# A weight transfer changes queue: the lower half of w_in's second piece goes to ScalarE's queue, and the gate weights go to GpSimd's

## The chip, the cores and the metric

The kernel runs on one core of a Trainium2 chip. A core has a matrix engine (TensorE, PE in the profile), a vector engine (VectorE, DVE), a scalar engine (ScalarE, ACT), a general engine (GpSimd, POOL) and an engine that only issues transfers and waits (SyncE, SP). Each has its own instruction stream, taken in order; they meet at semaphores. Transfers between the device memory and the on-chip memory are issued by instructions in the streams of SP, ACT or POOL, and are carried out by the core's 16 DMA engines.

The metric is the device time of one execution in microseconds (us).

## The reference: what is computed

Two branches read the same x (2048 tokens by 512 features, bf16), and a gate mixes them token by token:

```
g = sigmoid((x * gate_w).sum(-1))
a = linear attention of x: q, k, v = x @ wqkv; per head softmax features of q and k,
    kv = phi_k^T v, o = (phi_q kv) / (phi_q z), a = o @ wo
b = z = gelu(x @ w_in)  (2048 x 1376), split in z1 and z2; z2 is layer-normed,
    multiplied by the 2048 x 2048 matrix w_sp, plus b_sp; b = (z1 * that) @ w_out
out = g * a + (1 - g) * b
```

The change touches only how two inputs are brought in: `w_in` (512 x 1376) and `gate_w` (512 values).

## The kernel before, in words

The order of all work is written out by hand; the framework adds the semaphores. Tokens are worked in 16 tiles of 128. First comes z = x @ w_in for all tiles, with gelu on ScalarE and the statistics of the layer norm on VectorE; then the attention features and the large product with w_sp; then the outputs. The change and everything that the prediction speaks of lie in the first 20 us, in the z stage.

**What a z tile needs.** The contraction over 512 features is cut in four slices of 128 (`dt` 0 to 3). The 1376 columns of w_in are cut in three pieces: columns 0 to 511, 512 to 1023, and 1024 to 1375 with one further column F that holds the gate weights, so that the same matmuls also give x . gate_w. `z_piece` (L177, matmul at L180) does one piece of one tile. Tiles 0 and 1 are taken side by side and start early: their x comes by a plain load (L108, L109), is transposed on TensorE (`x_transpose`, L195) and copied out by VectorE for tile 0 (L204) and by ScalarE for tile 1 (L206). The other x tiles come by transposing transfers (L123, L129).

**The order on TensorE at the start** is: 24 matmuls on constants (`spin`, L189), the two x transposes, four more on constants, then for tiles 0 and 1 in turn, slice by slice: columns 0 to 255, columns 256 to 511, the gate column's small matmul (`gate_column`, L209), columns 512 to 1023. After that comes the third piece of tile 0, that of tile 1, and tiles 2 to 15. VectorE copies the four gate values of each row into column F of w_in (L212). This copy writes into the same tile as the third piece's load and is ordered behind it; the third piece's matmuls read column F and so wait for the copy.

**The transfers of w_in.** For short they have names here. Each is one call of `load_w_in` (L111), save d:

| name | what | KB | queue before |
|---|---|---|---|
| a, a' | columns 0-255, slices 0-1 and slices 2-3 | 128 each | SP, ScalarE |
| b, b' | columns 256-511, slices 0-1 and slices 2-3 | 128 each | SP, ScalarE |
| c, c' | columns 512-1023, slices 0-1 and slices 2-3 | 256 each | SP, SP (L119) |
| d | columns 1024-1375, all slices (L122) | 352 | SP |

SP's queue holds, in this order: x tile 0, a, b, c, c', d, the transposing load of x tiles 2 and 3 (L123), wv (L124), more x (L129), and so on. ScalarE's queue holds x tile 1, a', b', the gate weights gw (L120, 1 KB), and much later the outputs. After its transfers ScalarE runs a small gelu that loads its tables (L121). GpSimd's queue holds no transfer at all; GpSimd builds the identity (L101, L102), clears a part of w_out (L153), builds masks (L162 to L167) and clears paddings (L173, L174). VectorE's first instruction (L175) adds two halves of a mask and waits for L167.

**Completion counters.** The framework gives the transfers of the SP and ScalarE queues eight completion semaphores in turn. A ninth transfer takes the first one's, and its issue waits until that first one has landed. Before the change the eight are x tile 1, x tile 0, a', a, b', b, gw and c; so c' is the ninth and waits for x tile 1, and d the tenth, which waits for x tile 0.

Of the kernel before, what the change touches and what calls it, by code (L numbers as in the profile page):

```python
# [14 lines left out]
P = 128  # L15
# [9 lines left out]
CH = 512  # L25
# [14 lines left out]
def kernel(  # L40
# [14 lines left out]
    nc = tc.nc  # L55
# [11 lines left out]
    def zbank(t):  # L67
# [32 lines left out]
    gw = pers.tile([NDT, P], BF16, name="gw")  # L100
    nc.gpsimd.memset(ident[:], 1.0)  # L101
    nc.gpsimd.affine_select(  # L102
        out=ident[:], in_=ident[:], pattern=[[-1, P]],
# [7 lines left out]
    def load_w_in(eng, d0, d1, n0, n1):  # L111
        eng.dma_start(out=w_in[:, d0:d1, n0:n1], in_=w_in_v[:, d0:d1, n0:n1])  # L112

    HC = CH // 2
    for n0 in (0, HC):
        load_w_in(nc.sync, 0, 2, n0, n0 + HC)
        load_w_in(nc.scalar, 2, 4, n0, n0 + HC)
    for d0 in (0, 2):
        load_w_in(nc.sync, d0, d0 + 2, CH, 2 * CH)  # L119
    nc.scalar.dma_start(out=gw[:], in_=gate_w.rearrange("(dt p) -> dt p", p=P))  # L120
    nc.scalar.activation(out=st[:, 9, 0:1], in_=ones[:, 0:1], func=AF.Gelu_apprx_tanh)  # L121
    nc.sync.dma_start(out=w_in[:, :, 2 * CH:F], in_=w_in_v[:, :, 2 * CH:F])  # L122
    nc.sync.dma_start_transpose(out=xT[:, :, 2 * P:CH], in_=x2[2 * P:CH, :])  # L123
# [1 line left out]
        out=wv[:, :, :],  # L125
        in_=A_wqkv[:, 2 * D:3 * D].rearrange("(dt p) n -> p dt n", p=P),
    )
    for q in range(1, NCH):
        nc.sync.dma_start_transpose(  # L129
            out=xT[:, :, q * CH:(q + 1) * CH], in_=x2[q * CH:(q + 1) * CH, :]  # L130
        )
        if q == 1:
            nc.sync.dma_start(
                out=wphiW[:, :, :],
                in_=A_w_phi.rearrange("(g h) e f -> (h e) g f", g=NDT),
# [3 lines left out]
        out=bcolb[:, :, :], in_=B_b_sp.rearrange("(t p) -> t p", p=P)  # L139
# [7 lines left out]
    for t in range(WSLOTS):  # L147
        load_wsp(t)
    nc.sync.dma_start(
        out=w_out[:, 0:NFT - 1, :],  # L150
        in_=B_w_out[0:(NFT - 1) * P, :].rearrange("(ft p) n -> p ft n", p=P),
# [4 lines left out]
        out=w_out[0:last_m, NFT - 1, :], in_=B_w_out[(NFT - 1) * P:FH, :]  # L156
    )
    nc.sync.dma_start(
        out=wo[:, :, :], in_=A_wo.rearrange("(g p) n -> p g n", p=P)
# [4 lines left out]
        out=mask16[:], in_=mask16[:], pattern=[[-16, 8]],  # L164
# [3 lines left out]
        out=mask16[:], in_=mask16[:], pattern=[[16, 8]],  # L168
# [420 lines left out]
```

## Time and profile before

| | us |
|---|---|
| median of 3 runs | 208.01 (208.0 to 208.05) |
| the profiled execution | 208.12 |
| its span (first to last instruction) | 206.4 |
| TensorE busy in the span | 202.3 (98%) |
| VectorE busy | 148.5 (72%) |
| ScalarE busy | 82.1 (40%) |
| GpSimd busy | 49.5 (24%) |

The profile shows one execution. "Busy" is the sum of an engine's instructions; a group's line gives the code line, the engine, the operation, its tiles and its count. The chain is followed back from the last instruction, at each step to what released it. The timeline gives start, duration, engine and line; "SPq" and "ACTq" are transfer issues on the SP and ScalarE queues, and the time to landing in the list of transfers runs from the start of the issue until all of the data is there.

### The profile page before, as it was taken

To read this page: it belongs to the slowest core of one execution; us is meant where nothing else is said; L and a number is where in the kernel's file an instruction comes from. 1 tells how busy PE (TensorE), PEld (TensorE's weight loads), DVE (VectorE), ACT (ScalarE), POOL (GpSimd) and SP (SyncE) were. 2 spreads that over 40 slices of the span, in tenths; PEclk is the share of its full clock that TensorE was granted. 3 is DMA by queue.
4 is the path that set the end of the run, shared out by engine and by line. 5 is a ranking of instruction groups with operands and counts; after the bars stand their busy time and mean duration, and the time that the engine had idled before them with its cause. 6 is when DMAs were issued, how large, how long until landed. Compare 5 with 4: busy or idle time off the path is not lost.

```text
span 206.4 us, 3685 instructions
## 1 busy us (share of the span) xinstructions
PE 202.3 (98%) x1399; PEld 117.8 (57%) x1399; DVE 148.5 (72%) x304; ACT 82.1 (40%) x145; POOL 49.5 (24%) x46
## 2 busy tenths in 40 slices
PE   8999999999999999999999999999999999999994
PEld 8545555554455666666666667666455555555542
DVE  1049858385887888879898996798989788796500
ACT  4266767675684324250505102222524243341122
POOL 4000000000002353525352543032532252322000
PEclk9999999999999999999999999999999999999999
DMA  5999899997000638463757781145756974566451
GB/s 160 289 178 247 189 170 226 168 192 231 0 3 0 140 65 117 102 112 85 153 126 109 139 174 41 38 91 84 161 131 122 127 176 98 129 141 153 110 110 51
DMA packets 90378, 26.50 MB, mean 128 GB/s; under 512 B 84296, under 2 KB 90360, under 8 KB 90360
## 3 DMA queue, kind: packets, MB, share of 16 engines
q1 hardware_dynamic: 87360, 23.87, 60.2%
q10 hardware_dynamic: 3000, 2.39, 3.8%
q8 instruction: 11, 0.18, 0.4%
q14 instruction: 7, 0.06, 0.1%
HBM read 3.44 MB, written 2.10 MB: 27 GB/s over the span
## 4 chain that ended last, share of the span: by engine, by line
PE 96%; DMA 2%; SPq 0%; ACT 0%; issue 0%
PE ps L405 36%; PE ps L180 18%; PE ps L326 13%; PE ps L448 10%; PE ps L453 7%; PE ps L282 7%; DMA w_in<-in_B_w_in_dram 2%; PE ps L427 2%; PE ps L377 2%; PE ps L305 1%; SPq L112 0%; SPq L108 0%; ACT ob L457 0%; PE ps L209 0%
## 5 line engine op out<-in xcount | busy, mean ns | idle before, releaser
L405 PE MATMUL ps<-zz,wsp 128*128 128x344 bf16 x512 | 84.1, 309 | 0.0
L343 POOL TENSOR_TENSOR w_in<-w_in,rs 128x512 bf16<-128x512 bf16 x28 | 41.3, 1475 | 124.7 <-DVE rs L341 112.4
L405 PEld LDWEIGHTS <-wsp 128*128 128x128 bf16 x512 | 49.9, 98 | 28.1
L334 ACT ACTIVATE w_in<-ps 128x512 bf16<-128x512 f32 x56 | 30.1, 596 | 63.3 <-issue 21.4
L180 PE MATMUL ps<-w_in,xT 128*128 128x512 bf16 (+2 forms) x200 | 39.7, 350 | 0.4 <-DMA w_in<-in_B_w_in_dram 0.4
L339 DVE TENSOR_REDUCE zs<-w_in 128x64 f32<-128x1024 bf16 x28 | 33.8, 1209 | 0.0
L413 DVE SCALAR_TENSOR_TENSOR u<-ps,bcol,zz 128x344 bf16<-128x344 f32 x32 | 18.4, 574 | 18.6 <-PE ps L427 8.3
L180 PEld LDWEIGHTS <-xT 128*128 128x128 bf16 x200 | 19.1, 98 | 18.0 <-issue 0.8
L215 ACT ACTIVATE zz<-ps 128x1376 bf16<-128x1376 f32 (+2 forms) x18 | 21.4, 1190 | 18.6 <-PE ps L180 18.6
L448 PE MATMUL ps<-w_out,uT 128*128 128x512 bf16 (+2 forms) x102 | 23.5, 366 | 0.0
L224 DVE BATCH_NORM_STATS2 stats<-zz 128x6 f32<-128x344 bf16 x32 | 14.8, 505 | 11.1 <-ACT zz L215 11.1
L377 PE MATMUL ps<-vv,w_in 128*128 128x65 bf16 x128 | 21.7, 193 | 0.0
L343 DVE TENSOR_TENSOR w_in<-w_in,rs 128x512 bf16<-128x512 bf16 x28 | 19.4, 693 | 1.0
L341 DVE RECIPROCAL rs<-zs 128x64 f32<-128x64 f32 x32 | 17.7, 553 | 3.2
L457 ACT ACTIVATE ob<-ps 128x512 bf16<-128x512 f32 (+2 forms) x17 | 9.7, 572 | 25.1 <-PE ps L453 19.9
L453 PE MATMUL ps<-wo,oT 128*128 128x512 bf16 (+2 forms) x68 | 16.6, 366 | 0.0
L326 PEld LDWEIGHTS <-xT 128*128 128x128 bf16 x128 | 10.8, 98 | 9.9
L326 PE MATMUL ps<-wq,xT 128*128 128x512 bf16 x64 | 16.4, 379 | 0.0
L326 PE MATMUL ps<-wk,xT 128*128 128x512 bf16 x64 | 16.3, 379 | 0.0
L427 PE MATMUL ps<-kvx,wqkT 128*128 128x68 bf16 x128 | 15.8, 194 | 0.0
L282 PE MATMUL ps<-wv,xT 128*128 128x512 bf16 x64 | 15.6, 379 | 0.0
L448 PEld LDWEIGHTS <-uT 128*128 128x128 bf16 x102 | 9.5, 98 | 10.4
(56 smaller groups left out, 134.3 us busy)
## 6 DMA issues: line engine op xcount, KB each, us to landing
out_dram<-ob ACTq DMA_DIRECT2D x15, 128.0 KB, 2.1
w_out<-in_B_w_out_dram SPq DMA_DIRECT2D x1, 640.0 KB, 4.9
w_in<-in_B_w_in_dram SPq DMA_DIRECT2D x2, 256.0 KB, 4.5
wv<-in_A_wqkv_dram SPq DMA_DIRECT2D x1, 512.0 KB, 5.0
wo<-in_A_wo_dram SPq DMA_DIRECT2D x1, 512.0 KB, 5.3
w_in<-in_B_w_in_dram SPq DMA_DIRECT2D x1, 352.0 KB, 4.9
w_in<-in_B_w_in_dram ACTq DMA_DIRECT2D x2, 128.0 KB, 4.0
w_in<-in_B_w_in_dram SPq DMA_DIRECT2D x2, 128.0 KB, 3.6
```

Of the source, the lines that this page charges most:

```text
L180: nc.tensor.matmul(zb[:, n0:n1], lhsT=xT[:, dt, t * P:(t + 1) * P], rhs=w_in[:, dt, n0:n1], start=(dt == 0), stop=(dt == NDT - 1),)
L215: nc.scalar.activation(out=zz[:, t, n0:n1], in_=zbank(t)[:, n0:n1], func=AF.Gelu_apprx_tanh)
L282: nc.tensor.matmul(ps[:, b, :], lhsT=xT[:, dt, t * P:(t + 1) * P], rhs=wv[:, dt, :], start=(dt == 0), stop=(dt == NDT - 1),)
L326: nc.tensor.matmul(ps[:, b, :], lhsT=xT[:, dt, t * P:(t + 1) * P], rhs=w[:, dt, :], start=(dt == 0), stop=(dt == NDT - 1),)
L334: nc.scalar.activation(out=e[:, :, a, :], in_=src, func=AF.Exp, scale=sc)
L339: nc.vector.tensor_reduce(out=zs[:], in_=ev, axis=AX.X, op=ALU.add)
L343: eng.tensor_tensor(out=ev[:, sl, :], in0=ev[:, sl, :], in1=rs[:, sl, None].to_broadcast([P, H, DH]), op=ALU.mult,)
L377: nc.tensor.matmul(slots[:, g, 0:HW + 1], lhsT=ek_t[t][:, g, :, :].rearrange("p a n -> p (a n)"), rhs=vv[:, t, g, 0:HW + 1], start=(t == 0 ...
L405: nc.tensor.matmul(ps[:, b, 0:HF], lhsT=wsp[:, tt % WSLOTS, s, :], rhs=zz[:, s, FH + h * HF:FH + (h + 1) * HF], start=(s == 0), stop=(s == ...
L427: nc.tensor.matmul(slots[:, g, 0:QW], lhsT=eT_t[t][:, g, :], rhs=kvx[:, g, :], start=True, stop=True)
L448: nc.tensor.matmul(ps[:, b, n0:n1], lhsT=uT[:, ft, :], rhs=w_out[:, ft, n0:n1], start=(ft == 0), stop=False,)
L453: nc.tensor.matmul(ps[:, b, n0:n1], lhsT=oT[:, g, :], rhs=wo[:, g, n0:n1], start=False, stop=(g == NDT - 1),)
```

## The change

The second piece of w_in was loaded by two transfers on SP's queue. Now its upper half c stays there, and its lower half c' becomes the fourth transfer on ScalarE's queue, where gw stood. The gate weights are issued on GpSimd's queue, whose first transfer they are; in GpSimd's stream the issue stands behind the identity and ahead of L153.

```diff
     for n0 in (0, HC):
         load_w_in(nc.sync, 0, 2, n0, n0 + HC)
         load_w_in(nc.scalar, 2, 4, n0, n0 + HC)
-    for d0 in (0, 2):
-        load_w_in(nc.sync, d0, d0 + 2, CH, 2 * CH)
-    nc.scalar.dma_start(out=gw[:], in_=gate_w.rearrange("(dt p) -> dt p", p=P))
+    load_w_in(nc.sync, 0, 2, CH, 2 * CH)
+    load_w_in(nc.scalar, 2, 4, CH, 2 * CH)
+    nc.gpsimd.dma_start(out=gw[:], in_=gate_w.rearrange("(dt p) -> dt p", p=P))
     nc.scalar.activation(out=st[:, 9, 0:1], in_=ones[:, 0:1], func=AF.Gelu_apprx_tanh)
     nc.sync.dma_start(out=w_in[:, :, 2 * CH:F], in_=w_in_v[:, :, 2 * CH:F])
```

No arithmetic changes, and no transfer changes its size.

## The prediction

> **What bounds the kernel now.** The page's chain of what ended last comes first: 96% of the span is TensorE, 2% transfers, all of it w_in. So only what lets TensorE start or continue earlier can pay, and only in the stretch where it waits for w_in. The same chain in order of time, for the first 30 us, shows that stretch:
>
> ```profile
> 1.72 4.46 DMA w_in<-in_B_w_in_dram
> 6.18 0.04 issue
> 6.22 1.05 PE ps L180 x8
> 7.28 0.10 PE ps L209
> 7.38 12.50 PE ps L180 x64
> ```
>
> TensorE waits until 6.18 for one transfer issued at 1.72 (b), and from 6.22 on the chain stays on TensorE. The waits of the same window say how much idle time that is, and where else w_in is waited for:
>
> ```profile
> DVE w_in L212 <- DMA w_in<-in_B_w_in_dram: 4.1, 1, 4.1
> PE ps L180 <- DMA w_in<-in_B_w_in_dram: 0.4, 1, 0.4
> PEld L180 <- DMA w_in<-in_B_w_in_dram: 0.2, 1, 0.2
> SPq L112 <- DMA xn<-in_A_x_dram: 0.8, 1, 0.8
> ```
>
> TensorE is idle 0.43 us ahead of b. The gate column's copy on VectorE waits for d. SP's issue of c' waits 0.8 us for an x tile (the ninth transfer's counter). The timeline of the issues, and the transfers with their time to landing:
>
> ```profile
> 1.73 0.51 ACTq L112 DMA_DIRECT2D w_in<-in_B_w_in_dram  x1
> 2.27 0.62 ACTq L120 DMA_DIRECT2D gw<-in_gate_w_dram  x1
> ...
> 2.22 0.47 SPq L112 DMA_DIRECT2D w_in<-in_B_w_in_dram  x1
> ...
> 3.54 0.37 SPq L112 DMA_DIRECT2D w_in<-in_B_w_in_dram  x1
> ...
> 3.96 0.47 SPq L122 DMA_DIRECT2D w_in<-in_B_w_in_dram  x1
> 4.47 1.95 SPq L123 DMA_TRANSPOSE xT<-in_A_x_dram  x1
> ```
>
> ```profile
> w_in<-in_B_w_in_dram SPq DMA_DIRECT2D x1, 256.0 KB, 4.8
> w_in<-in_B_w_in_dram SPq DMA_DIRECT2D x1, 128.0 KB, 4.5
> w_in<-in_B_w_in_dram ACTq DMA_DIRECT2D x1, 128.0 KB, 4.9
> ...
> w_in<-in_B_w_in_dram SPq DMA_DIRECT2D x1, 352.0 KB, 4.9
> w_in<-in_B_w_in_dram SPq DMA_DIRECT2D x1, 256.0 KB, 4.3
> ```
>
> Issue plus time to landing: b 6.18, b' 1.73 + 4.9 = 6.63, c 2.22 + 4.8 = 7.02, c' 3.54 + 4.3 = 7.84, d 3.96 + 4.9 = 8.86. Against this the needs on TensorE. The second piece's matmuls start at 7.31 and then every 0.216 us (8 of them, two a slice): c is needed at 7.31, c' (slices 2 and 3) at 7.31 + 4 x 0.216 = 8.17. The third piece could start at 7.31 + 8 x 0.216 = 9.04; it starts at 9.19, because VectorE's copy, released by d, runs from 8.96 to 9.14. So there are 0.29 us of slack on c, 0.33 on c', and 0.15 us of waiting behind d. The last line to read is the rate of the 16 DMA engines, by stretches:
>
> ```profile
> 3.50:5.50 2.00, 2.00 (x20) 1.82 (x19) 0.82 (x3) 1.63 (x5) 0.00 (x0) 1.00 0.93 244
> 5.50:6.60 1.10, 0.67 (x7) 0.45 (x6) 0.00 (x0) 0.00 (x0) 0.00 (x0) 1.00 1.00 314
> 6.60:7.00 0.40, 0.40 (x5) 0.33 (x4) 0.00 (x0) 0.00 (x0) 0.00 (x0) 1.00 1.06 358
> ```
>
> The third number from the right is the granted clock, the next the busy share of the DMA engines, the last GB/s: they are full (0.93 to 1.06) when c, c' and d move. The wait is for bytes, not for an issue.
>
> **The change, part by part.**
>
> SP's queue loses c' (0.37 us of issue). Without gw on the ScalarE queue, the first eight counters are x tile 1, x tile 0, a', a, b', b, c' and c: none of these waits, and d is now the ninth, released by x tile 1's landing. So d is issued at 3.54 instead of 3.96 and all that SP issues behind it (x tiles 2 and 3, wv, the later x, w_phi, wqk) up to 0.42 us earlier. With the DMA engines full until d has landed, an earlier issue brings no earlier byte: 0. The x tiles 2 and 3 land at 4.47 + 5.4 = 9.87, ahead of their first use at 9.19 + 8 x 0.15 = 10.39; those 0.52 us cover them, and without them a later landing would count in full. wv is first read at 19.72.
>
> ScalarE's queue loses gw (0.62 us of issue) and gains c' (0.46 to 0.51, the rows of its own w_in issues): its table load starts about 0.13 us earlier, at 2.79 for 2.92. Its next work, tile 1's copy at 4.45, waits for the transposes on TensorE, which end at 4.41: 0. SP had four transfers out (x, a, b, c) before any had landed, so a fourth on ScalarE's queue need not block its stream.
>
> c' enters its queue at 2.27 instead of 3.54, behind b' and no longer behind c. This is the edit that counts. From 6.63, when b' is down, c needed 0.39 us more, then c' 0.82 (256 KB, 320 GB/s), then d 1.02. Now c and c' run together. If the engines alternate between the two queues, c takes 2 x 0.39 and lands at 7.41, 0.39 later; c' has 0.43 us of work left, shares with d, and lands at 7.41 + 0.86 = 8.27, 0.43 later; d, whose engines have moved the same bytes in all, lands at 8.86 as before. On TensorE: c at 7.41 moves the second piece's start from 7.31 to 7.45 (0.04 from landing to start, as at b), 0.14 late; c' is then needed at 8.31 and there at 8.27 + 0.04; the second piece ends at 9.18, and the third starts at 9.19 behind the copy, as now. The delay goes where the wait behind d was: 0. I add 0.05 for an unequal division, since this balance has no slack left. Bounds: if the new c' simply stays behind, c lands at 7.02 and nothing is lost; if ScalarE's queue is served first, c' lands at 7.45 and c at 7.84: start 7.88, 0.57 late, less 0.15 = 0.42. If both queues finish together at 8.27, it is 1.00 - 0.15 = 0.85. I stay with alternation because b and b', issued 0.01 us apart, landed within 0.45 us of each other.
>
> The Trainium skill, "DMA: Bandwidth & Descriptors", section "Queues, rings and completion order", says that each DMA engine takes its queues in turn, a packet at a time; by that rule c ends at 7.41, by the trace's sequence without sharing at 7.02. The same page, section "Issuing engines are not separate DMA queues", speaks against the change: several issuing engines save issue time alone, so the sum would be no gain. The full DMA engines of the rows above agree.
>
> gw goes to GpSimd, at about 1.40, behind the identity (L102 ends at 1.36). No row prices a GpSimd issue: the other queues' issues go from 0.34 (an output) to 1.95 (a transpose); I take gw's own 0.62, the same transfer. Landing runs from 2.5 (x tile, nothing ahead) to 4.9 (b'). Early: 1.40 + 2.5 = 3.9. Late: 1.40 + 1.95 + 4.9 = 8.25. I take the x tiles' 2.7 with the issue beside it, 1.40 + 0.62 + 2.7 = 4.7, since gw is alone on its queue as they were. TensorE reads it at 7.20: 2.5 us of cover, so 0; at the late bound it costs 8.29 - 7.20 - 0.15 = 0.94. The GpSimd work behind it (masks, clears) slips by the issue: L175, VectorE's first instruction, starts at 2.43 and stands in front of tile 0's copy at 4.03, so 1.6 us of GpSimd issue are covered; at 1.95 the copy would start 0.35 late, inside the 0.43 us in which TensorE waits for b. The Trainium skill, page "DMA: Bandwidth & Descriptors", section "Anatomy of one DMA — SWDGE (gpsimd) path", puts the fixed cost of such a transfer at some 2.0 us; by it an estimate of the landing would be 3.4, and no row here shows one.
>
> The end: SP waits for all counters; GpSimd's makes one more. Between the last landing (203.90 + 1.5 = 205.4) and the end of the span there is 1.0 us of such waits and barriers, eleven counters in all; one more is 0 to 0.1, taken as 0.05.
>
> Sum: 0 + 0.05 + 0 + 0.05 = +0.1 on the profiled execution's 208.12, that is 208.2. This execution stands 0.11 above the median of the runs, 208.01, so the prediction for the median is 208.1.
>
> **The rivals.** (1) *Hidden altogether*: c keeps its 7.02 and only issue moves. For it: c' had 0.33 us of slack and d sets the third piece. Against it: full DMA engines. 208.0. (2) *c becomes the wait*, slower: TensorE reads slices 0 and 1 first, but now slices 2 and 3 compete with them. It decides once c lands after 7.31 + 0.15 + 0.42 - 0.04 = 7.84, the bound above. For it: the balance has no reserve, and 244 GB/s in 3.5 to 5.5 against 358 later shows slowed engines while both queues were in use. +0.42 to +0.85: 208.4 to 208.9. (3) *gw is late*: it decides from a landing at 7.7 on; up to +0.94, 208.95. Against it: 2.5 us of cover. (4) *Faster*: the hole at 244 GB/s goes with the order in which SP hands out c', d and the transposes; moved, it may spare b. At 358 GB/s those 2 us would move the same bytes in 1.36. The gain is capped by what TensorE waits, 0.43 + 0.15 = 0.58: 207.4. Against it: b and b' are issued before the first changed transfer, and both queues were already in use while b moved.
>
> **How the numbers follow.** 0.2% (0.42 us) is about what a measurement of this kernel can tell from no change. Chances: the forecast 0.42 (its own range 208.0 to 208.3), hidden 0.14, c the wait 0.22, gw late 0.08, faster 0.14. From these: same 0.56, slower 0.30, faster 0.14. The range goes from 207.6, within rival 4, to 208.8, within rivals 2 and 3; about 0.1 is left out on each side.
>
> **What the profile of the changed kernel would show.** d issued near 3.54; c' issued on ACTq near 2.27, the table load near 2.8; c landing near 7.4 and c' near 8.3 where before they were 0.82 apart; a small new wait of L180 for w_in at 7.3 to 7.5; L212 still near 8.96; third piece near 9.19; L209 without a wait for gw; L175 before 4.03. The prediction is wrong if b lands away from 6.18, if L180 waits over 0.5 us at the second piece, or if L209 waits.

## The result, and the profile after

The changed kernel takes 208.58 us (median of 17 runs) against 208.05 us of the kernel before (17 runs beside it). The ratio is 1.0024, with a 95% interval of 1.0016 to 1.0031: slower by about 0.50 us. The profiled execution took 208.56 us with a span of 206.8 us, where the one before took 208.12 and 206.4. Two executions of the experiments below that ran at a lower granted clock (215.57 us at 0.984 in the run with the lower half late, 359.45 us at 0.66 in the run with the lower half entering 1 us later) are left out of their ratios.

The chain in order of time, for the first 30 us of the changed kernel (start, duration, what):

```profile
2.23 5.49 DMA w_in<-in_B_w_in_dram
7.72 0.04 issue
7.76 0.38 PE ps L180
```

Before, the transfer in the chain was b, issued at 1.72 and down at 6.18. Now it is c, issued at 2.23 and down at 7.72. The waits of the same window, and the transfers in flight near 2.2 us with their time to landing:

```profile
DVE w_in L212 <- DMA w_in<-in_B_w_in_dram: 4.0, 1, 4.0
DVE mask L175 <- POOL mask L167: 3.3, 1, 3.3
PE ps L180 <- DMA w_in<-in_B_w_in_dram: 0.9, 2, 0.5
```

```profile
w_in<-in_B_w_in_dram SPq DMA_DIRECT2D x1, 256.0 KB, 5.5
w_in<-in_B_w_in_dram ACTq DMA_DIRECT2D x1, 256.0 KB, 5.6
w_in<-in_B_w_in_dram SPq DMA_DIRECT2D x1, 128.0 KB, 4.3
w_in<-in_B_w_in_dram ACTq DMA_DIRECT2D x1, 128.0 KB, 4.6
gw<-in_gate_w_dram POOLq DMA_DIRECT2D x1, 1.0 KB, 3.3
```

TensorE now waits twice for w_in, 0.9 us in all: 0.44 for b (0.43 before), and 0.51 for c. The issues of c and c' are 0.05 us apart (2.23 and 2.28), and they land 0.19 us apart, at 7.72 and 7.91. Before they were 0.81 apart, at 7.02 and 7.83. The lower half gained nothing; the upper half, which is read first, lost 0.70. The gate weights landed at 1.43 + 3.3 = 4.7, long before their use near 7.1.

Where the time went can be followed exactly, because TensorE never waits for a transfer again. The second piece starts at 7.76 instead of 7.31 (0.45 late). The third piece starts at 9.49 instead of 9.19, since d still lands at 8.88 and the copy L212 still runs at 8.96: 0.15 us of the delay went into the wait that had stood there. From there on, TensorE is 0.30 us late up to the end of the kernel, as the last issue of an output shows, at 203.90 before:

```profile
204.20 0.34 ACTq L458 DMA_DIRECT2D out_dram<-ob  x1
```

The span grew by 0.48, so 0.18 us came at the very end. In the trace's records of that stretch, the last output needs 0.03 longer to land; from landing to the meeting of all engines it is 0.34 instead of 0.27 (SP has one wait instruction more, for GpSimd's counter); and the closing work of GpSimd, its drains and the clearing of the semaphores, takes 0.08 longer.

### The profile page after: what moved, and what is told of

Its sections match the earlier page's. It is cut to its first block, busy times and chain, and to the rows that moved or that the text cites. A ratio compares the mean times of both kernels' runs of the same rounds, so it can differ in the third digit from the quotient of the medians.

```text
span 206.8 us, 3664 instructions
## 1 busy us (share of the span) xinstructions
PE 200.8 (97%) x1376; PEld 117.4 (57%) x1399; DVE 148.6 (72%) x304; ACT 82.1 (40%) x145; POOL 49.9 (24%) x47
## 4 chain that ended last, share of the span: by engine, by line
PE 94%; DMA 3%; issue 1%; SPq 1%; ACT 0%
PE ps L405 36%; PE ps L180 17%; PE ps L326 13%; PE ps L448 10%; PE ps L282 7%; PE ps L453 7%; DMA w_in<-in_B_w_in_dram 3%; PE ps L427 2%; PE ps L377 2%; PE ps L305 1%; SPq L112 0%; SPq L108 0%; ACT ob L457 0%
## 5 line engine op out<-in xcount | busy, mean ns | idle before, releaser
L180 PE MATMUL ps<-w_in,xT 128*128 128x512 bf16 (+2 forms) x197 | 39.4, 349 | 1.1 <-DMA w_in<-in_B_w_in_dram 0.9
L180 PEld LDWEIGHTS <-xT 128*128 128x128 bf16 x200 | 19.0, 97 | 18.5 <-issue 1.1
L326 PE MATMUL ps<-wk,xT 128*128 128x512 bf16 x57 | 15.7, 379 | 0.3
L326 PE MATMUL ps<-wq,xT 128*128 128x512 bf16 x57 | 15.6, 379 | 0.3
L282 PE MATMUL ps<-wv,xT 128*128 128x512 bf16 x61 | 15.5, 379 | 0.2
```

The lines of the kernel that those rows point to most:

```text
L180: nc.tensor.matmul(zb[:, n0:n1], lhsT=xT[:, dt, t * P:(t + 1) * P], rhs=w_in[:, dt, n0:n1], start=(dt == 0), stop=(dt == NDT - 1),)
L282: nc.tensor.matmul(ps[:, b, :], lhsT=xT[:, dt, t * P:(t + 1) * P], rhs=wv[:, dt, :], start=(dt == 0), stop=(dt == NDT - 1),)
L326: nc.tensor.matmul(ps[:, b, :], lhsT=xT[:, dt, t * P:(t + 1) * P], rhs=w[:, dt, :], start=(dt == 0), stop=(dt == NDT - 1),)
```

## The experiments

Two theories were set against each other first. S, sharing: c' on ScalarE's queue enters the DMA engines together with c and takes half of them, so c is late. G: GpSimd's first transfer is what disturbs the head. Each run is given as the ratio of its time to that of the kernel before, with a 95% interval. In all runs the landing is of the slowest of the 16 engines; "L282" is the start of the first weight load of v_proj (19.57 before), which carries the delay of the head unmixed with the end. Each profile is one execution, and the head scatters from one to the next: b, issued at 1.72 to 1.75 in every run but the one with one queue, landed anywhere from 5.21 to 7.19, and L282 came 0.35 early in the run on the price at the end, which only moves the gate weights and loads them twice. So a shift of L282 by 0.3 us in one profile proves little; what carries the argument is the order of landings, the waits and the packets.

**The gate weights on GpSimd's queue alone** (against the kernel before)

```diff
     for d0 in (0, 2):
         load_w_in(nc.sync, d0, d0 + 2, CH, 2 * CH)
-    nc.scalar.dma_start(out=gw[:], ...)
+    nc.gpsimd.dma_start(out=gw[:], ...)
```

> One part alone: gw is issued on GpSimd's queue, c' stays on SP's queue. Theory S (sharing: c' on ScalarE's queue competes with c for the DMA engines, c lands late and TensorE waits for it) expects the head of the kernel as before: c about 0.8 us ahead of c', no wait of L180 for w_in at the second piece, first v_proj matmul (L282) near 19.7; only the end grows by the 0.18 us that the span of the changed kernel has beyond the 0.30 us shift of everything else. Ratio 1.0009. Rival G (GpSimd's transfer disturbs the head) expects the whole: L282 0.3 us later and a ratio of 1.0024.

Measured: 1.0010 (0.9996 to 1.0023), which alone tells little; the profile tells it. Its transfers on either side of 2.2 to 2.75 us:

```profile
w_in<-in_B_w_in_dram SPq DMA_DIRECT2D x1, 256.0 KB, 4.7
...
w_in<-in_B_w_in_dram SPq DMA_DIRECT2D x1, 256.0 KB, 4.9
```

c landed at 2.23 + 4.7 = 6.9 and c' at 2.75 + 4.9 = 7.67. L180 did not wait for w_in at the second piece, and L282 came at 19.54, 0.03 early. From the start of the last matmul to the end of the span it is 3.20 us, where it was 3.02 before and 3.20 in the changed kernel. So the 0.18 at the end comes with the move of gw to GpSimd's queue, and nothing of the 0.30 at the head does: G falls.

**The lower half on ScalarE's queue alone, gw on SP's** (against the kernel before)

```diff
-    for d0 in (0, 2):
-        load_w_in(nc.sync, d0, d0 + 2, CH, 2 * CH)
-    nc.scalar.dma_start(out=gw[:], ...)
+    nc.sync.dma_start(out=gw[:], ...)
+    load_w_in(nc.sync, 0, 2, CH, 2 * CH)
+    load_w_in(nc.scalar, 2, 4, CH, 2 * CH)
```

> The other part alone: c' is on ScalarE's queue, gw is on SP's queue between b and c, and GpSimd issues nothing. S expects the wait for c to stay: c and c' land within 0.4 us of each other near 7.7 to 7.9, L180 idle 0.3 to 0.6 us ahead of the second piece, L282 0.2 to 0.45 us later than before, no growth at the end; ratio 1.0010 to 1.0020. Rival G expects the kernel before: ratio 1.000.

Measured: 1.0013 (1.0001 to 1.0026), L282 0.21 late, the end at 3.02 as before. The time is inside what S gave, but the landings are not, and it came about in another way. gw took a counter, so c became the ninth transfer and was issued at 3.63; c' (issued at 2.28) landed first, at 6.91, and c at 7.63. TensorE waited 0.48 us for c. In this run the half that entered first landed first; it could not show sharing, so the next run has no transfer of gw.

**The lower half on ScalarE's queue, no transfer of the gate weights**

```diff
-    nc.gpsimd.dma_start(out=gw[:], ...)
+    nc.gpsimd.memset(gw[:], 0.0)
```

(against the changed kernel)

> c' on ScalarE's queue as changed, and no transfer of the gate weights at all: GpSimd clears gw instead, so the gate values are left out of the result. The run before this with c' alone had also delayed the issue of c by a counter wait; here c is issued near 2.2 with nothing in front. Theory S (c and c' share the DMA engines from b' on) expects c and c' to land within 0.3 us of each other between 7.5 and 7.9, L180 idle 0.4 to 0.6 us, L282 0.2 to 0.4 us later than before, the end as before (3.0 us from the last matmul); ratio 1.0010 to 1.0020. Rival G (GpSimd's transfer matters for the head) expects c near 7.0 and ratio 1.000.

Measured: 1.0037 (1.0023 to 1.0050), L282 0.68 late. The two halves among its transfers (the last column is the time to landing):

```profile
w_in<-in_B_w_in_dram SPq DMA_DIRECT2D x1, 256.0 KB, 5.9
w_in<-in_B_w_in_dram ACTq DMA_DIRECT2D x1, 256.0 KB, 6.0
```

and TensorE's waits for w_in (sum, number, longest):

```profile
PE ps L180 <- DMA w_in<-in_B_w_in_dram: 0.9, 2, 0.7
```

Again 0.19 us apart, at 8.10 and 8.29, with no GpSimd transfer in the program: S stands. Both landed later than expected (7.5 to 7.9), and the wait of 0.7 and the ratio are above what was expected; b came at 5.99, but b' (6.74 for 6.30 in the changed kernel) and all transfers from there down to d (9.28 for 8.88) were later in this execution. The ratio is no smaller than that of the whole change, so the two parts do not simply add up across these runs; their intervals overlap.

**The halves exchanged between the queues** (against the changed kernel)

```diff
-    load_w_in(nc.sync, 0, 2, CH, 2 * CH)
-    load_w_in(nc.scalar, 2, 4, CH, 2 * CH)
+    load_w_in(nc.sync, 2, 4, CH, 2 * CH)
+    load_w_in(nc.scalar, 0, 2, CH, 2 * CH)
```

> As changed, but the halves change queues: ScalarE's queue loads c (read first), SP's queue loads c'. S in its plain form (the two queues share evenly) expects the same wait: c lands within 0.2 us of 7.7, ratio 1.0020 to 1.0030. Rival Q (ScalarE's queue runs behind SP's, since its first packets started 0.4 us later) expects c later than c' and a longer wait, 0.2 to 0.4 us more than the changed kernel: ratio 1.003 to 1.005. If ScalarE's queue is served first, c lands near 7.0 and the wait is gone.

Measured: 1.0035 (1.0022 to 1.0047). The half on SP's queue (now c') landed at 7.67, the one on ScalarE's (now c) at 7.86: 0.19 apart once more. TensorE's wait before the second piece was 0.9 us, because b happened to land at 5.33 and TensorE came to the second piece sooner. L282 is 0.44 late against 0.30, of which the later landing of c makes 0.14. So both forms were partly right: the two queues share evenly, and ScalarE's comes out 0.2 behind whatever it carries. The packets of the two queues (q1 is SP's, q10 ScalarE's) between 5.6 and 6.6 us show the sharing itself, in the kernel before:

```profile
q1 hardware_dynamic: 334, 0.30, 93.2%
q10 hardware_dynamic: 46, 0.02, 6.9%
```

in the changed kernel:

```profile
q10 hardware_dynamic: 215, 0.20, 57.4%
q1 hardware_dynamic: 210, 0.18, 51.7%
```

and with the halves exchanged:

```profile
q1 hardware_dynamic: 183, 0.15, 50.4%
q10 hardware_dynamic: 177, 0.17, 48.4%
```

(packets, MB, share of the 16 engines' time). Before, SP's queue had the engines nearly to itself in the stretch in which c is completed; after, it has half. Since landings scatter, c is best measured from b: the run with one queue aside, it landed 0.44 to 1.25 us after b in the seven profiles in which c was issued at 2.2 to 2.7 us and c' not with it, and 1.65, 2.11 and (here) 2.53 us after b in the three in which c' was issued with it.

**Everything on one queue**

```diff
         load_w_in(nc.sync, 0, 2, n0, n0 + HC)
-        load_w_in(nc.scalar, 2, 4, n0, n0 + HC)
+        load_w_in(nc.sync, 2, 4, n0, n0 + HC)
```

(against the kernel before)

> The contrary of the change: all of w_in on SP's queue in the order a, a', b, b', c, c', d, only x tile 1 and gw on ScalarE's. S, with the DMA engines full, expects every load to land in the order in which it is read: b near 5.9, b' 6.5, c 7.0, c' 7.8, d 8.85, so TensorE waits less for b and the same for d: ratio 0.9990 to 1.0. Rival H (two queues in use at once are what slowed the engines to 244 GB/s between 3.5 and 5.5 us) expects that hole to close: d up to 0.6 us earlier, ratio 0.997 to 0.9985. If issue time on SP counts, a' and b' come late instead: slower, 1.002.

Measured: 1.0019 (1.0009 to 1.0030), slower. b and b' came sooner, as S said (b at 5.59 for 6.18, b' 5.98 for 6.63) and c at 7.02; but c' landed at 8.31 and d at 9.35, 0.5 us later than before, and the third piece waited for it. H falls: with one queue, 3.5 to 5.5 us moved 216 GB/s, less than the 244 of two. The DMA engines had idle time there (the next to last number is their busy share; first the kernel before, then this run):

```profile
3.50:4.50 1.00, 1.00 (x12) 1.00 (x11) 0.47 (x3) 0.95 (x3) 0.00 (x0) 1.00 0.96 230
3.50:4.50 1.00, 1.00 (x14) 0.95 (x13) 0.42 (x3) 0.14 (x1) 0.00 (x0) 1.00 0.69 156
```

So here the second queue is worth having. The rival of issue time had forecast the ratio, and one issue of 128 KB took 0.46 to 0.47 us with 0.04 between, which is 128 KB in 0.51, or 257 GB/s at most. But of the two pieces that it expected late only a' was (5.22 for 4.34), so that issue time is what was short is argued, not shown.

**The lower half late on ScalarE's queue** (against the changed kernel)

```diff
-    load_w_in(nc.scalar, 2, 4, CH, 2 * CH)
-    nc.gpsimd.dma_start(out=gw[:], ...)
+    nc.scalar.dma_start(out=gw[:], ...)
...
         x_copy(1, d0, d1)
+    load_w_in(nc.scalar, 2, 4, CH, 2 * CH)
```

> c' stays on ScalarE's queue but is issued later, behind tile 1's copies (near 5.2 instead of 2.28), when most of c has moved; gw is on ScalarE's queue as before. If sharing with c is the whole cost (S), c lands near 7.0 again and L180 does not wait for it; c' is then shared with d and lands between 7.6 and 8.4, so a wait of 0 to 0.3 us may stand at slice 2 instead; L282 within 0.15 us of before, ratio 0.9995 to 1.0010. Rival R (whatever loads c' on ScalarE's queue costs, whenever it is issued) expects the wait of 0.45 us for c to stay, ratio 1.0015.

Measured: 1.0221 (1.0182 to 1.0259), far off. Half of S came true: c landed at 6.46 and nothing waited for it, though c' was on ScalarE's queue, so R falls. But c', issued at 5.52, landed at 11.0, and TensorE waited 3.2 us for it. ScalarE's queue stood nearly still meanwhile; the packets from 5.6 to 7.6 us:

```profile
q1 hardware_dynamic: 1257, 0.53, 118.1%
q10 hardware_dynamic: 3, 0.00, 0.2%
```

Then SP's transposing load of x tiles 2 and 3 was through, and from 7.8 to 8.8 us q10 moved 209 packets. L282 came 4.40 late, more than the wait of 3.2. Much of the rest goes with TensorE's granted clock, which was 0.50 after that wait (the third number from the right):

```profile
11.20:14.60 3.40, 3.40 (x11) 1.51 (x10) 0.13 (x1) 1.12 (x3) 0.00 (x0) 0.50 0.75 151
```

**The second piece by slices over both queues** (against the changed kernel)

```diff
-    load_w_in(nc.sync, 0, 2, CH, 2 * CH)
-    load_w_in(nc.scalar, 2, 4, CH, 2 * CH)
-    nc.gpsimd.dma_start(out=gw[:], ...)
+    load_w_in(nc.sync, 0, 1, CH, 2 * CH)
+    load_w_in(nc.scalar, 1, 2, CH, 2 * CH)
+    nc.sync.dma_start(out=gw[:], ...)
+    load_w_in(nc.sync, 2, 3, CH, 2 * CH)
...
         x_copy(1, d0, d1)
+    load_w_in(nc.scalar, 3, 4, CH, 2 * CH)
```

> Both queues load the second piece, but in the order in which it is read: slice 0 on SP's and slice 1 on ScalarE's queue first (128 KB each), then gw and slice 2 on SP's, and slice 3 on ScalarE's behind tile 1's copies. S expects that the order of need is what counts: slices 0 and 1 land near 7.0 and slices 2 and 3 near 7.9, no wait at the second piece, d as before, the end as before: ratio 0.9995 to 1.0005, no better than before since d and the copy still set the third piece. Rival R (two queues for the second piece cost) expects 1.0015.

Measured: 1.0096 (1.0072 to 1.0120). Slices 0 and 1 landed at 6.26 and 6.07, slice 2 at 7.27: the order of need, as S says. Slice 3 was issued at 6.20, moved no packet between 6.3 and 8.4, and landed at 10.22; TensorE waited 1.7 us for it. With slice 3 issued earlier, behind the table load:

```diff
     nc.scalar.activation(out=st[:, 9, 0:1], ...)
+    load_w_in(nc.scalar, 3, 4, CH, 2 * CH)
```

> The second piece by slices over both queues in the order of need (slices 0 and 1 first, then 2 and 3), with slice 3 issued right behind ScalarE's table load, near 4.3, so that it is issued before SP issues the transposing load of x tiles 2 and 3; in the run with slice 3 behind that load it moved no packet until the load was through. GpSimd issues nothing. Theory S (order of need) with this: slices 0 and 1 land at 6.0 to 6.4 as there, slices 2 and 3 at 7.2 to 8.0, nothing waits at the second piece, tile 1's copies start up to 0.3 us late under the wait for b, the end as before; L282 within 0.15 us of before and the ratio 0.9990 to 1.0005. If a fourth transfer on ScalarE's queue issued after 4 us is late in itself, slice 3 lands after 9 and the ratio is 1.004 to 1.010 as there.

Measured: 1.0054 (1.0036 to 1.0072). Slice 3, issued at 4.22, landed at 8.20, so a fourth transfer on that queue is not late in itself. TensorE did not wait for the second piece, but d came at 9.27 and L282 0.40 late. The profiled execution took 208.33 us, well under the median of 209.25, so its profile does not account for the time; where the rest goes stays open.

**When does a transfer on ScalarE's queue stand still?** Two further runs put wv ahead of the transposing load on SP's queue, gw on ScalarE's, and c' on ScalarE's queue once behind the table load and once ahead of it (the cuts show only where c' stands):

```diff
     nc.scalar.activation(out=st[:, 9, 0:1], ...)
+    load_w_in(nc.scalar, 2, 4, CH, 2 * CH)
```

> c' on ScalarE's queue issued between the two tried (2.28 and 5.5): right behind the table load, near 4.4; gw on ScalarE's queue as before; on SP's queue wv goes ahead of the transposing load of x tiles 2 and 3, so that this load is issued after c' (its tiles come late by that, which TensorE pays at tile 2, near 10: the time is no verdict on c'). Theory S: c lands between the 6.5 of the late issue and the 7.7 of the early one, 6.5 to 7.2. Theory T (a copy on ScalarE's queue that is issued behind a transposing load on SP's moves nothing until that load is through): c' lands at 7.3 to 8.5, since no such load is in front. Rival N (late issue on ScalarE's queue is slow in itself, 5.5 us to landing): c' lands near 9.9.

```diff
     nc.scalar.dma_start(out=gw[:], ...)
+    load_w_in(nc.scalar, 2, 4, CH, 2 * CH)
     nc.scalar.activation(out=st[:, 9, 0:1], ...)
```

> As the run with c' issued at 4.16, with one difference: c' stands ahead of ScalarE's table load, so that it is issued near 3.6 and ahead of SP's wv (issued at 3.83 there), with wv and the transposing load of x tiles 2 and 3 behind it on SP's queue in the same order. ScalarE's table load and tile 1's copies come about 1 us late by that, and x tiles 2 and 3 late as there, so the time is no verdict. Theory L (a transfer on ScalarE's queue waits for what SP has issued before it to get into the queues, so a big SP transfer ahead of it in time of issue holds it up): c' now moves right behind b' and lands between 7.5 and 8.5; c, with c' beside it again, lands at 6.8 to 7.8. Rival N (a transfer issued late on ScalarE's queue takes 5 to 7 us in itself): c' lands at 9 to 11.

Each ran once (211.20 and 210.09 us). In the first, c' was issued at 4.16, ahead of the transposing load (4.41), and yet landed at 11.40: T falls in the form given, and so does the 9.9 of N. From 5.6 to 7.4 us its queue moved 10 packets, and SP's 641. c landed at 7.66, outside the 6.5 to 7.2 that S gave; b had landed at 7.19 in this execution, so all of the head was late. In the second, c' was issued only 0.50 us earlier, at 3.66, but ahead of d (3.86) and wv (4.29):

```profile
w_in<-in_B_w_in_dram ACTq DMA_DIRECT2D x1, 256.0 KB, 3.7
```

It landed at 7.37, a little earlier than L's 7.5 to 8.5: 3.7 us after its issue instead of 7.2. N falls, as the early slice 3 above had already shown, and L, that a transfer waits for what the other queue has issued ahead of it, is borne out by this pair. It is still only argued as a mechanism: no view shows the unit that hands out the packets. c landed at 6.63, below L's 6.8 to 7.8 and 0.74 ahead of c'; c' was issued 1.35 us after it.

**The lower half on ScalarE's queue, entering 1 us after the upper** (against the changed kernel)

```diff
-    load_w_in(nc.sync, 0, 2, CH, 2 * CH)
-    load_w_in(nc.scalar, 2, 4, CH, 2 * CH)
-    nc.gpsimd.dma_start(out=gw[:], ...)
+    nc.sync.dma_start(out=gw[:], ...)
+    load_w_in(nc.sync, 0, 2, CH, 2 * CH)
     nc.scalar.activation(out=st[:, 9, 0:1], ...)
+    load_w_in(nc.scalar, 2, 4, CH, 2 * CH)
```

> c' stays on ScalarE's queue but enters it some 1.2 us after c enters SP's instead of 0.05 us: gw goes to SP's queue ahead of c (which takes c from 2.23 to near 2.65), the table load follows b' at once, and c' is issued behind it near 3.8, ahead of tile 1's copies and ahead of SP's transposing load (near 4.3). GpSimd issues nothing. Theory S (what delays c is a c' that enters together with it) expects c 0.3 to 0.8 us ahead of c', c at 6.8 to 7.3, no wait of L180 at the second piece above 0.1 us, c' at 7.4 to 8.2, the end as before (3.0 us): L282 within 0.2 us of before, ratio 0.9990 to 1.0010; the gain cannot pass the 0.15 us that the third piece waits behind d's landing. Rival R (c' on ScalarE's queue costs wherever it enters) expects the wait of 0.4 to 0.7 us for c as in the changed kernel: ratio 1.0015 to 1.0035.

Measured: 1.0005 (0.9988 to 1.0022), no difference from the kernel before that can be told. The transfers issued from 2.2 to 4.0 us:

```profile
w_in<-in_B_w_in_dram SPq DMA_DIRECT2D x1, 256.0 KB, 3.8
w_in<-in_B_w_in_dram ACTq DMA_DIRECT2D x1, 256.0 KB, 4.4
```

c was issued at 2.71 and landed at 6.55, c' at 3.71 and 8.10. L180 waits for no w_in at all, and the end is 3.05. R falls by the missing wait; the time alone could not tell, since its interval overlaps that of the changed kernel. This is the cleanest showing of S: the queue and the bytes of c' are those of the change, and it enters 1.00 us after c instead of 0.05 (gw, 1 KB, is on SP's queue). c and c' ended further apart than the 0.8 expected. L282 is 0.22 late for another reason, told in the last section below.

**The price at the end by itself** (against the kernel before)

```diff
+    gw2 = pers.tile([NDT, P], BF16, name="gw2")
+    nc.gpsimd.dma_start(out=gw2[:], ...)
```

(beside gw on GpSimd's queue, c' on SP's)

> c' on SP's queue as before; gw on GpSimd's queue, and a second transfer of the same weights on it into a tile that nothing reads. It measures the 0.18 us at the end by itself. If it is the price of using the queue at all (one more wait instruction, since waits go in pairs, and slower drains on GpSimd), the stretch from the last matmul's start to the end of the span is 3.18 to 3.20 us, as with one transfer. If it goes with each transfer, it is near 3.36.

Measured, in one execution: 3.20 us, the same as with one transfer. So the price does not go with each transfer. In the runs with GpSimd's queue this stretch was 3.18 to 3.21; in those without it 2.89 to 3.11, as SP had two to five waits. The run without a transfer of gw, with 3.11, also has the fifth wait, though GpSimd issues nothing there: that part, 0.07, comes with one more counter, whoever uses it. Only the 0.08 in GpSimd's closing work is found in every run with its queue and in none without.

## Why the prediction was right, and where it was not

The measured 208.58 lies in the range of 207.6 to 208.8, and the change was slower, as 0.30 of the chances had it. But the sum, +0.1, was too small by a factor of five, and its likeliest case (208.0 to 208.3) did not come. What happened is nearest to its second rival, in that c became the wait, but not as that was written: it was to decide once c landed after 7.84 and to cost 0.42 to 0.85 at the head, and c landed at 7.72 and the head lost 0.30. That the total lies in this rival's 208.4 to 208.9 is luck, made by the 0.18 at the end. By the prediction's own sign, a wait of L180 over 0.5 us at the second piece, it was wrong at that step: the wait was 0.51. Point by point:

- *What bounds the kernel* held. The engines were full, the earlier issue of d (3.76 for 3.96, not the 3.54 forecast: x tile 1 landed at 3.74) brought d no sooner: 8.88 both times. L209 did not wait; L175 moved to 3.28, within its cover; the table load moved by 0.12 (0.13 forecast), for nothing.
- *c lands at 7.41* is the step that failed. It was worked out by letting c' join c only at 6.63, when c had 0.39 us of work left. That 6.63 is the landing on the slowest engine; before the change the first of the 16 was through with b' at 4.93, 1.7 us earlier, and there c' could begin at once beside c. In the packet records of the changed kernel, c's first packet moved at 4.69 and the first of c' at 4.90 (of SP's and ScalarE's transfers between the x tiles and wv, only c and c' move in packets of 1 KB). So c was shared nearly from its start: 7.72, and c' came at 7.91 instead of the 8.27 forecast. The mechanism, alternation of two queues, was right, and its start was wrong; the term of the sum was 0 for the head with 0.05 added, and measured 0.30. The bounds of 7.02 and 7.84 that stood beside it did hold the measured landing. The Trainium skill's rule ("DMA: Bandwidth & Descriptors", section "Queues, rings and completion order", engines take their queues in turn) agrees with the packet counts above, 210 to 215; from the moment that both halves are queued it gives two landings close together, as measured. The Trainium skill's other rule, in the section "Issuing engines are not separate DMA queues" of the same page, that several issuing engines save issue time alone, agrees with the changed kernel, where the second queue brought d no earlier; in the run with one queue, though, the engines stood partly idle, and d came 0.47 us later.
- *The absorption* of 0.15 behind d came out exactly (0.45 became 0.30).
- *The end* was put at 0.05 between 0 and 0.1, from a count of the waits. It measured 0.18: 0.07 for the wait as thought, but 0.08 more in GpSimd's closing work, and 0.03 in the landing. The bound was wrong, since it priced only SP's side.
- *gw on GpSimd*: issue 0.70 us (0.62 taken), landing 4.73 (4.7 taken). The 2.0 us that the Trainium skill states as the fixed cost ("DMA: Bandwidth & Descriptors", section "Anatomy of one DMA — SWDGE (gpsimd) path") was too short here: 3.3 us from the start of the issue, with the DMA engines full.
- *The hole in the DMA rate* from 3.5 to 5.5 us was read by rival 2 as two queues in use, by rival 4 as the order in which SP hands out c', d and the transposes. The run with one queue made it deeper (216 GB/s for 244). With c' moved it was 267, and b landed 0.11 earlier, but TensorE came to it 0.10 earlier and waited as long. The cause of the hole stays open.

## What to carry to other kernels

In these runs, transfers on two queues did not come one after the other but together: moving the half that is needed second to a second queue delays the half that is needed first, even when no byte is added and both engines' issue is free. Check what the earlier one loses, not only what the moved one gains. Letting the transfers enter in the order of need took the wait away here, but no such run was faster than the kernel before, where d and the copy behind it set the time. A queue that was unused so far also has a price at the end of the program, and when some engines run ahead of others, the landing that a trace shows is that of the slowest one, which is no time at which sharing begins.

## What the runs showed of the hardware that was not expected

A transfer on ScalarE's queue can stand still for 2 to 3 us while SP's queue moves: 3 packets against 1257 in 2 us. It was so when SP had issued the transposing load or the 512 KB of wv shortly before it (issued at 4.16, 5.52 and 6.20: landing 7.2, 5.5 and 4.0 us later), and not so when it was issued at 3.66, ahead of them (3.7 us). By these runs the order of issue across queues counts, not only the order within one.

SP's transposing load also holds back what is complete. In the trace's records of the kernel before, 358 of d's 512 packets had moved by 7.5 us and the last moved at 8.38, while its counts on all sixteen engines arrived only between 8.81 and 8.88, when packets of the transposing load that had stood from 7.6 on got going. It was so in every run in which that load was issued within 0.7 us after d: all counts came within 0.15 us. In the run with c' issued at 4.16, where wv stands between the two, the counts came one by one, from 7.28 to 8.74. Even there the landing is that of the slowest engine.

In the run with the lower half entering 1 us later, TensorE had no wait for w_in and was late all the same. x tile 0 landed at 3.69, after the matmuls on constants had ended, so TensorE stood idle ahead of the transposes:

```profile
3.74 1.03 PE L195 MATMUL ps<-ident,xn 128*128 128x128 bf16 x8 [0.18 <-DMA xn<-in_A_x_dram]
4.56 0.63 PE L189 MATMUL ps<-const-bfloat16-1.0 128*128 128x128 bf16 x4
4.99 2.64 PE L180 MATMUL ps<-w_in,xT 128*128 128x256 bf16 x16
```

The 16 matmuls of 256 columns took 2.64 us; up to 6.48 they started 0.21 us apart, then 0.11, with a granted clock of 1.00 in all of that time. Before, 8 of them took 1.05. The idle time is not the cause of the double spacing: it stands from the first matmul on in every profile, where the 24 matmuls on constants start 0.105 us apart (0.055 in the second set of the changed kernel). What differs is when it ends: near 4.0 in the changed kernel, 4.85 before, 6.48 here, and 6.12 in the run with the gate weights alone, whose TensorE had no gap until then. So this run was late because x tile 0 came late and because the double spacing lasted longer; neither has to do with c'. The Trainium skill, "TensorE: Matmul & The Clock Gate", section "Part 1: The HAM clock gate (the "warmup" mystery)", states that TensorE runs at half rate by default and again after an idle window of some 3.4 us, and at full rate after some 3.4 us of sustained work. The spacing here agrees with half and full rate, though the column of the granted clock does not show it. In the run with the lower half late the column does: after 3.17 us without a matmul the granted clock was 0.50 for 3.41 us, from 11.23 on; after 2.10 us, in the run with c' issued at 4.16, it stayed at 1.00.
